# Buffers of their own for the shared loads of a Hyena filter and max-out FFN kernel

## The chip, the core and the metric

The kernel runs on one core of a Trainium2 chip. The metric is the device time of one execution in microseconds (us), the median of several executions. A core has TensorE (PE: matmuls and their weight loads), VectorE (DVE), ScalarE (ACT) and GpSimd (POOL); SyncE (SP) does no arithmetic here and issues most of the transfers. On-chip memory is SBUF; matmuls write to PSUM.

## The reference

Two blocks, one behind the other. The first is a Hyena filter: a small network makes a filter of 12544 positions for each of 128 channels, and the product u = x v of two inputs is convolved with it along the sequence, for 4 batches, by a Fourier transform of twice the length. The second is a feed-forward block with a maximum of three projections.

```python
def _attn_ref(x, v, pos_emb, w1, w2):
    B, S, D = x.shape                       # 4, 12544, 128
    h_mlp = np.maximum(pos_emb @ w1, 0.0) @ w2
    h_filt = h_mlp * np.exp(-0.01 * np.arange(S, dtype=np.float32))[:, None]
    u = x * v
    L = 2 * S
    y = irfft(rfft(u, n=L) * rfft(h_filt, n=L)[None], n=L)[:, :S, :]   # along the sequence
    return x * y

def _moe_ref(x, w1, w2, w3, w_out):         # x: 50176 x 128, d_ff 768
    h = np.maximum(np.maximum(x @ w1, x @ w2), x @ w3)
    return h @ w_out
```

## The kernel before

The transform is done as matmuls. For one batch the work of the convolution is cut into 32 *units* (a piece of both inputs: multiply, turn, first transform) and then 45 *tables* (a pair of frequencies: second transform, product with the filter's spectrum, and the transform back). The convolution of batch b + 1 runs beside the feed-forward block of batch b, step by step in one written order (`manual_schedule`: nothing is reordered). A step, or slot, is one up projection of 392 tokens, 192 steps to a batch.

This is where the conv work of the next batch is put. `s` is the slot in which a unit is joined, or a table's second transform is done; `late` 1 puts an entry behind those with 0 in its slot.

```python
    def conv_steps(b, done):
        ...
        per_pair = 165 / (NK + 0.6 * (NU - done))          # NK = 45 tables, NU = 32 units
        for u in range(done, NU):                          # done: 6 for batch 1, else 0
            s = (u - done) * 0.6 * per_pair + 12
            at(max(0, int(s) - 11), 0, u_load, b, u)
            at(int(s) - 7, 0, u_mul, u)
            at(int(s) - 6, 0, u_planes, u)
            at(int(s) - 5, 0, u_dma, u)
            at(int(s), 0, u_join, u)
            for h in range(2):
                at(int(s + 2 + 0.3 * per_pair * h), 1, u_first, u, h)
        s0 = int((NU - done) * 0.6 * per_pair) + 13
        for g in range(NK):
            s = s0 + int(g * per_pair)
            at(s - 5, 0, w_load, g, 0)
            at(s - 3, 0, h_load, g)
            at(s, 1, g_second, g)
            at(s + 1, 0, g_butterfly, g)
            at(s + 1, 0, w_load, g, 1)
            at(s + 2, 1, g_swap, g)
            at(s + 3, 0, g_re, g)
            at(s + 4, 0, g_im, g)
            at(s + 5, 0, g_sum, g, nc.gpsimd)
            at(s + 7, 0, g_unfold, g)
            at(s + 8, 1, g_third, b, g)
            at(s + 9, 0, g_pair, g)
            at(s + 10, 0, g_store, b, g, nc.gpsimd)
```

The pieces and the buffers that they use. A tile with the same tag in the same pool shares that tag's `bufs` buffers in turn. Unit inputs and tables share the tags `u0` and `u1` of the pool `inq`; a unit's planes share `x` with the spectra `xt`, the turned planes share `xs` with the swapped spectra.

```python
    def u_load(b, u):                                      # xr -> u0, vr -> u1
        ...
            t = pool.tile([P, 512 if pool is inq else 4 * NB], FP32, tag=f"u{len(ts)}", name="ut")
            ...
            nc.sync.dma_start(t, src[4 * g0:4 * g0 + 4, :, c, b, :].rearrange("g p n -> p g n"))
    def u_mul(u):
        a, v = us[u]
        nc.vector.tensor_tensor(out=a, in0=a, in1=v, op=ALU.mult)
    def u_planes(u):                                       # halves of the floats, on GpSimd
        pl_ = cvp.tile([P, 2, 4, P], U16, tag="x", name="planes", bufs=state["xb"])
        ...
    def u_dma(u):                                          # transpose by DMA
        t = cvp.tile([P, 8, P], U16, tag="xs", name="turned", bufs=state["xsb"])
        nc.sync.dma_start_transpose(out=t[:], in_=us.pop(u)[:].rearrange("p h s n -> p (h s n)"))
    def u_join(u): ...                                     # uT <- turned: one half ACT, one DVE
    def u_first(u, h, copy=None): ...                      # matmuls ps <- f, uT; spec <- ps

    def w_load(g, a):                                      # table a = 0 second, 1 third transform
        w = inq.tile([P, 512], FP32, tag=f"u{a}", name="wt")
        nc.sync.dma_start(w[:], wt_d[g, :, a, :])
    def h_load(g): ...                                     # the filter's spectrum, tag uT, SyncE
    def g_butterfly(g):                                    # DVE, writes xt
        xt = state["cv"][0].tile([P, 2, 2, D], FP32, tag="x", name="xt", bufs=state["xb"])
    def g_swap(g):                                         # ACT, xs <- xt
        xs = state["cv"][0].tile([P, 2, 2, D], FP32, tag="xs", name="xs", bufs=state["xsb"])
    def g_re(g): ...                                       # DVE, xt = xt * ht
    def g_im(g): ...                                       # DVE, xs = xs * ht
    def g_sum(g, eng): ...                                 # POOL, xt = xt + xs
    def g_unfold(g):                                       # DVE, ab <- xt
        y = xts.pop(g)
        ab = state["cv"][0].tile([P, 2, 2, D], FP32, tag="ab", name="ab", bufs=2)
        for q, op in enumerate((ALU.add, ALU.subtract)):
            nc.vector.tensor_tensor(out=ab[:, :, q, :], in0=y[:, :, 0, :], in1=y[:, :, 1, :], op=op)
    def g_third(b, g): ...                                 # PE, ps <- ab, wt; then ACT z1 <- ps
```

The pools of the main part, and the step itself:

```python
    hp = ctx.enter_context(tc.tile_pool(name="hp", bufs=3))
    inq = ctx.enter_context(tc.tile_pool(name="inq", bufs=4))     # left over, nothing in it
    utp = ctx.enter_context(tc.tile_pool(name="utq", bufs=3))
    ...
    inq = ctx.enter_context(tc.tile_pool(name="inq", bufs=2))     # the one that is used
    cvp = ctx.enter_context(tc.tile_pool(name="cvp", bufs=3))
    ...
    state = {"turn": cps, "cv": (cvp, cps), "xb": 4, "xsb": 4}

        for j, (name, f) in enumerate(ORDER):              # 12 steps for a pair of token tiles
            if j in loads: bring(k + 1, loads.index(j))    # zt and xT of the next pair, SyncE
            h[name, f] = up(...)                           # pa, relu on ACT; pb, maximum on DVE
            ...
            run(stream.pop(step, ()))                      # down products (ops), sums on GpSimd
            if j in lasts ...: t_last(...)                 # yps, then gt <- yps, xT on DVE
            run(beside.pop(i * NF + j, ()))                # the convolution of the next batch
            step += 1
```

Of the kernel before, what the change touches and what calls it, by code (L numbers as in the profile page):

```python
# [9 lines left out]
FP32 = mybir.dt.float32  # L10
# [5 lines left out]
P = 128  # L16
# [54 lines left out]
def kernel(  # L71
# [16 lines left out]
    NG, _, _, B, NB = x.shape  # L88
    FO, S = posT.shape
    D = w2.shape[1]  # L90
# [226 lines left out]
    inq = None  # L317
# [7 lines left out]
    def pools(b, u):  # L325
        if b == 0:
            return inp0 if u % 2 else inp
        return inp if b == 1 and u < EARLY else inq

    def u_load(b, u):  # L330
        c, g0 = divmod(u, NG // 4)
        ts = []
        for src in (xr, vr):
            pool = pools(b, u)
            t = pool.tile([P, 512 if pool is inq else 4 * NB], FP32, tag=f"u{len(ts)}", name="ut")
            t = t[:, 0:4 * NB].rearrange("p (g n) -> p g n", g=4)
            nc.sync.dma_start(
                t, src[4 * g0:4 * g0 + 4, :, c, b, :].rearrange("g p n -> p g n"))
            ts.append(t)
        us[u] = ts  # L340
# [51 lines left out]

    def w_load(g, a):

        w = inq.tile([P, 512], FP32, tag=f"u{a}", name="wt")
        nc.sync.dma_start(w[:], wt_d[g, :, a, :])
        ws[g, a] = w[:].rearrange("p (k r m) -> p k r m", k=2, r=2)

# [38 lines left out]

    def g_unfold(g):
        y = xts.pop(g)
        ab = state["cv"][0].tile([P, 2, 2, D], FP32, tag="ab", name="ab", bufs=2)  # L440
        for q, op in enumerate((ALU.add, ALU.subtract)):
            nc.vector.tensor_tensor(out=ab[:, :, q, :], in0=y[:, :, 0, :], in1=y[:, :, 1, :],  # L442
                                    op=op)
        abs_[g] = ab
# [30 lines left out]
    def conv_steps(b, done):  # L475


        out = []

        def at(slot, late, fn, *args):  # L480
            out.append((slot, late, len(out), fn, args))

        per_pair = 165 / (NK + 0.6 * (NU - done))
        for u in range(done, NU):
            s = (u - done) * 0.6 * per_pair + 12
            at(max(0, int(s) - 11), 0, u_load, b, u)
            at(int(s) - 7, 0, u_mul, u)
            at(int(s) - 6, 0, u_planes, u)  # L490
            at(int(s) - 5, 0, u_dma, u)
            at(int(s), 0, u_join, u)
            for h in range(2):
                at(int(s + 2 + 0.3 * per_pair * h), 1, u_first, u, h)
# [16 lines that stand above are left out]
        slots = {}  # L511
        for s, _, _, fn, args in sorted(out, key=lambda r: r[:3]):
            slots.setdefault(s, []).append((fn, args))
        return slots
# [194 lines left out]
    warm_up(60)  # L709
    raws.append(load_raw(*jobs[0], nc.sync))  # L710
    u_load(0, 0)
    u_load(0, 1)
    raws.append(load_raw(*jobs[1], nc.sync))
    for u in range(2, 6):
# [11 lines left out]
    for f in range(0, FO, 4):  # L726
        quad([hs[:, f + i] for i in range(4)], f1h[:], specH[:, :, :, f:f + 4])
        u, k = divmod(f // 4, 4)
# [10 lines left out]
    for u in range(0, NU, 2):  # L739
        t = uts.pop(u)  # L740
        for v in range(2):
            if u + 4 < NU:
                u_mul(u + 4 + v)
            at = 4 * (u + v)
# [17 lines left out]
    cvp = pro.enter_context(tc.tile_pool(name="cvp0", bufs=3))  # L762
    cps = pro.enter_context(tc.tile_pool(name="cps0", bufs=3, space=PSUM))
    gps = pro.enter_context(tc.tile_pool(name="gps", bufs=2, space=PSUM))
    sps = pro.enter_context(tc.tile_pool(name="sps", bufs=1, space=PSUM))
    state = {"cv": (cvp, cps), "turn": cps, "xb": 2, "xsb": 2}
    pl = sps.tile([D, 512], FP32, name="pl")
    Gs = {}

# [41 lines left out]
    for s in range(NK + 3):  # L811
# [15 lines left out]
        if 2 <= s <= NK + 1:  # L827
            g_re(s - 2)
            g_im(s - 2)
            g_sum(s - 2, nc.vector)  # L830
            g_unfold(s - 2)
# [28 lines left out]
    inq = ctx.enter_context(tc.tile_pool(name="inq", bufs=4))  # L860
    utp = ctx.enter_context(tc.tile_pool(name="utq", bufs=3))
    f4p = hp.tile([N1, 2, NB // 2], FP32, name="f4p", bufs=1)
    nc.scalar.dma_start(f4p[:], f4p_d)
    inq = ctx.enter_context(tc.tile_pool(name="inq", bufs=2))
    cvp = ctx.enter_context(tc.tile_pool(name="cvp", bufs=3))
    cps = ctx.enter_context(tc.tile_pool(name="cps", bufs=3, space=PSUM))
    hps = ctx.enter_context(tc.tile_pool(name="hps", bufs=3, space=PSUM))
    ops = ctx.enter_context(tc.tile_pool(name="ops", bufs=1, space=PSUM))
    state = {"turn": cps, "cv": (cvp, cps), "xb": 4, "xsb": 4}
    banks = [ops.tile([P, 512], FP32, name=f"ops{i}") for i in range(2)]  # L870


# [25 lines left out]
    for k, (b, i) in enumerate(pairs):  # L898
        if i == 0:
            beside = {}  # L900
            if b + 1 < B:
                beside = conv_steps(b + 1, EARLY if b == 0 else 0)
# [68 lines left out]
```

## Time and profile before

| | |
|---|---|
| time, median of three | 2494.89 us (2493.93 to 2495.22) |
| span of the profiled execution | 2483.4 us |
| mean granted TensorE clock | 0.994 |
| DMA, mean | 165 GB/s |
| feed-forward steps | from 317 us on |

All times in the profile count from the start of the span. A line of the waits reads: engine, line of the kernel that waited, what ended the wait, then the total in us, how often, and the longest. A line of the table by stretches has, for each engine, its busy time and in brackets its instructions. Names such as `ps<-ab,wt` are the tile that is written and those that are read. "issue" means that the profile shows nothing that was waited for. The queue of SyncE is called SPq: its instructions are the issues of transfers, taken in order.

### The profile page before, as it was taken

The numbers are of one execution on the slowest core, as the hardware profiler recorded it, in microseconds if no ns is written. First come the engines' busy times: TensorE is split into PE (matmuls) and PEld (weight loads), VectorE is DVE, ScalarE is ACT, GpSimd is POOL, SyncE is SP. The second block draws the span as 40 slices with busy tenths as digits, with TensorE's granted clock in tenths as the row PEclk, the third lists the DMA queues.
The fourth block names the chain that finished last, engine by engine and source line by source line (L and its number), as shares of the span: only waits on it lengthen the run. The fifth ranks groups of instructions, "written<-read, shape, count | busy, mean of one in ns | idle before, by whom it ended". The sixth has DMA issues, their size and how long they took to land.

```text
span 2483.4 us, 70518 instructions
## 1 busy us (share of the span) xinstructions
PE 2370.5 (95%) x29025; PEld 1650.3 (66%) x29025; DVE 1623.6 (65%) x3044; ACT 1007.7 (41%) x1981; POOL 1388.5 (56%) x1595
## 2 busy tenths in 40 slices
PE   9999999999999899999999999998999999999999
PEld 8988867766666566666666666765666666666665
DVE  5588756576777747668887855658878873333333
ACT  2688834434334324434443423443344432222222
POOL 2022246566656666646665667646666665555565
PEclk9999999999999999999999999999999999999999
DMA  7789879767677559957877749966877853222221
GB/s 171 173 251 277 248 160 190 152 181 205 177 192 209 155 119 201 181 132 204 216 199 197 209 114 178 185 148 176 215 204 200 211 136 91 51 67 60 54 73 21
DMA packets 459274, 408.66 MB, mean 165 GB/s; under 512 B 322660, under 2 KB 338333, under 8 KB 458953
## 3 DMA queue, kind: packets, MB, share of 16 engines
q1 hardware_dynamic: 417664, 315.23, 53.9%
q0 software_dynamic: 28464, 75.72, 10.9%
q10 hardware_dynamic: 12825, 13.21, 1.7%
q8 instruction: 228, 3.74, 0.6%
q14 instruction: 93, 0.76, 0.1%
HBM read 295.76 MB, written 84.67 MB: 153 GB/s over the span
## 4 chain that ended last, share of the span: by engine, by line
PE 81%; DVE 11%; issue 3%; DMA 2%; ACT 1%; POOL 1%; SPq 0%; DVEq 0%; POOLq 0%; ACTq 0%
PE pa L131 17%; PE pb L131 17%; PE ops L622 17%; PE ps L131 12%; PE ps L140 7%; DVE ab L442 5%; PE yps L131 5%; PE sps L796 3%; DVE hid L576 2%; DVE zs L468 1%; DVE xt L430 1%; DVE xs L433 1%; PE pm L304 1%; PE gps L782 1%; PE pst L349 1%
## 5 line engine op out<-in xcount | busy, mean ns | idle before, releaser
L576 DVE TENSOR_TENSOR hid<-hid,pb 128x392 f32<-128x392 f32 x768 | 428.5, 558 | 504.3 <-PE pb L131 434.2
L573 ACT ACTIVATE hid<-pa 128x392 f32<-128x392 f32 x768 | 382.1, 497 | 715.0 <-PE pa L131 694.4
L131 PE MATMUL pa<-gt,w_sb 128*64 128x392 f32 x3072 | 642.0, 496 | 0.5 <-DVE hid L576 0.4
L131 PE MATMUL pb<-gt,w_sb 128*64 128x392 f32 x3072 | 639.0, 494 | 3.0 <-ACT hid L573 3.0
L131 PEld LDWEIGHTS pb<-gt,w_sb 128*64 128x64 f32 x3072 | 221.0, 137 | 293.7 <-issue 268.3
L622 PE MATMUL ops<-hid,wo_sb 128*64 128x196 f32 x3072 | 330.3, 328 | 0.0
L647 POOL DMA_DIRECT2D out_dram<-o x256 | 162.0, 637 | 280.5 <-DVE o L642 110.3
L622 PEld LDWEIGHTS ops<-hid,wo_sb 128*64 128x64 f32 x3072 | 220.2, 136 | 138.3 <-issue 113.8
L131 PE MATMUL ps<-ab,wt 128*64 128x128 f32 x2880 | 205.0, 280 | 86.9 <-DVE ab L442 84.1
L592 POOL TENSOR_TENSOR s<-hid 128x392 f32<-128x392 f32 x192 | 206.7, 1076 | 135.9 <-DVE hid L576 109.6
L592 POOL TENSOR_TENSOR s<-hid,s 128x392 f32<-128x392 f32 x192 | 201.0, 1047 | 99.3 <-DVE hid L576 97.2
L442 DVE TENSOR_TENSOR ab<-xt 128x256 f32<-128x256 f32 x360 | 252.2, 740 | 1.6
L131 PEld LDWEIGHTS ps<-ab,wt 128*64 128x64 f32 x2880 | 161.3, 137 | 130.8 <-DVE ab L442 110.2
L592 POOL TENSOR_TENSOR hid<-hid,s 128x392 f32<-128x392 f32 x192 | 204.8, 1073 | 42.9 <-DVE hid L576 24.5
L436 POOL TENSOR_TENSOR xt<-xt,xs 128x512 f32<-128x512 f32 x135 | 172.2, 1275 | 96.6 <-DVE xs L433 80.2
L131 PEld LDWEIGHTS pa<-gt,w_sb 128*64 128x64 f32 x3072 | 200.5, 138 | 21.2 <-issue 2.0
L430 DVE TENSOR_TENSOR xt<-xt,ht 128x512 f32<-128x512 f32 x180 | 201.7, 1121 | 14.3 <-ACT ht L801 14.1
L592 POOL TENSOR_TENSOR hid<-hid 128x392 f32<-128x392 f32 x192 | 203.2, 1077 | 0.2
L131 PE MATMUL ps<-spec,wt 128*64 128x128 f32 x2880 | 190.1, 274 | 2.1 <-issue 2.1
L140 PE MATMUL ps<-f,uT 98*64 98x90 f32 x4096 | 188.0, 242 | 4.3 <-DVE spec L144 3.1
L140 PEld LDWEIGHTS ps<-f,uT 98*64 98x64 f32 x4096 | 176.7, 137 | 13.6 <-ACT spec L144 4.0
L622 PE MATMUL ops<-s,tw 128*64 128x196 f32 x1536 | 170.8, 329 | 0.0
(105 smaller groups left out, 3067.7 us busy)
## 6 DMA issues: line engine op xcount, KB each, us to landing
wt<-wt_const SPq DMA_DIRECT2D x360, 256.0 KB, 4.6
ht<-hd SPq DMA_DIRECT2D x270, 256.0 KB, 5.0
zd<-zs POOLq DMA_DIRECT2D x135, 256.0 KB, 4.0
zt<-zd SPq DMA_DIRECT2D x192, 180.0 KB, 4.1
ut<-in_xr_dram SPq DMA_DIRECT2D x128, 196.0 KB, 3.5
ut<-in_vr_dram SPq DMA_DIRECT2D x128, 196.0 KB, 4.0
xT<-in_x_dram SPq DMA_DIRECT2D x256, 98.0 KB, 4.1
out_dram<-o POOLq DMA_DIRECT2D x256, 98.0 KB, 3.3
```

The source lines that it names most:

```text
L131: nc.tensor.matmul(out[64 * h:64 * h + 64], lhsT[:, 64 * h:64 * h + 64], rhs, start=start, stop=stop, skip_group_check=True)
L140: nc.tensor.matmul(ps[64 * c:64 * c + 64, 256 * i + r * N1:256 * i + (r + 1) * N1], a[:, r, :], table[:, c * N1:(c + 1) * N1], start=(i % ...
L304: nc.tensor.matmul(ps[64 * h:64 * h + HH, 512 * r + q * FO:512 * r + (q + 1) * FO], posv[64 * h:64 * h + 64, P - 1 - 2 * (8 * i + q) - r, ...
L430: nc.vector.tensor_tensor(out=xt[:], in0=xt[:], in1=hts[g][:, 0], op=ALU.mult)
L436: eng.tensor_tensor(out=xts[g][:], in0=xts[g][:], in1=xss.pop(g)[:], op=ALU.add)
L442: nc.vector.tensor_tensor(out=ab[:, :, q, :], in0=y[:, :, 0, :], in1=y[:, :, 1, :], op=op)
L573: nc.scalar.activation(h[:], pa[:, 0:N], Relu)
L576: nc.vector.tensor_tensor(out=h[:], in0=h[:], in1=pb[:, 0:N], op=ALU.max)
L592: nc.gpsimd.tensor_tensor(out=out[:], in0=a[:], in1=b[:], op=op)
L622: nc.tensor.matmul(ps[64 * c:64 * c + 64, 0:H2], w, rhs[:, :, c, :], start=start, stop=True, skip_group_check=True)
L647: nc.gpsimd.dma_start(dst[64 * m:64 * m + 64, 4 * i + c:4 * i + 8:2, b, :], t[m][64 * c:64 * c + 64].rearrange("d k (q n) -> d (k q) n", q=2))
L796: nc.tensor.matmul(ps[64 * h:64 * h + 64, (2 * c + k) * 2 * D:(2 * c + k + 1) * 2 * D], G[:, k, c], w2x[:].rearrange("p s d -> p (s d)"), ...
```

## The change

The tags `u0` and `u1` get four and three buffers in place of two each, and the pool that had nothing in it is no longer opened beside the one in use (its four was what the writer had meant to have). That takes 7 x 2 KB in place of 4 x 2 KB in each partition. It is paid for by one buffer less for `x` and for `xs` (three in place of four, 2 KB each) and one for `ab` (one in place of two, 2 KB). So that three buffers of planes last, a unit's steps from load to transpose come one slot later. The aim is that SyncE's queue, which takes its entries in order, no longer stands before a load whose buffer is in use. The arithmetic stays as it was; the prologue keeps its two buffers of `ab`.

```diff
 def u_load(b, u):
-            t = pool.tile([P, 512 if pool is inq else 4 * NB], FP32, tag=f"u{len(ts)}", name="ut")
+            t = pool.tile([P, 512 if pool is inq else 4 * NB], FP32, tag=f"u{len(ts)}", name="ut",
+                          bufs=4 - len(ts) if pool is inq else 3)
 def w_load(g, a):
-        w = inq.tile([P, 512], FP32, tag=f"u{a}", name="wt")
+        w = inq.tile([P, 512], FP32, tag=f"u{a}", name="wt", bufs=4 - a)
 def g_unfold(g):
-        ab = state["cv"][0].tile([P, 2, 2, D], FP32, tag="ab", name="ab", bufs=2)
+        ab = state["cv"][0].tile([P, 2, 2, D], FP32, tag="ab", name="ab",
+                                    bufs=state["abb"])
 def conv_steps(b, done):
-            at(max(0, int(s) - 11), 0, u_load, b, u)
-            at(int(s) - 7, 0, u_mul, u)
-            at(int(s) - 6, 0, u_planes, u)
-            at(int(s) - 5, 0, u_dma, u)
+            at(max(0, int(s) - 10), 0, u_load, b, u)
+            at(int(s) - 6, 0, u_mul, u)
+            at(int(s) - 5, 0, u_planes, u)
+            at(int(s) - 4, 0, u_dma, u)
 # prologue
-    state = {"cv": (cvp, cps), "turn": cps, "xb": 2, "xsb": 2}
+    state = {"cv": (cvp, cps), "turn": cps, "xb": 2, "xsb": 2, "abb": 2}
 # main part
-    inq = ctx.enter_context(tc.tile_pool(name="inq", bufs=2))
-    state = {"turn": cps, "cv": (cvp, cps), "xb": 4, "xsb": 4}
+    state = {"turn": cps, "cv": (cvp, cps), "xb": 3, "xsb": 3, "abb": 1}
```

## The prediction

> **What bounds the kernel now.** I read, in this order: the engine table of the page, the table by stretches, TensorE's waits, the waits of the DMA queue that SyncE issues on, VectorE's waits, and one stretch of the timeline. The first question is how much time TensorE is not working, since nothing else can be won.
>
> ```profile
> PE 2370.5 (95%) x29025; PEld 1650.3 (66%) x29025; DVE 1623.6 (65%) x3044; ACT 1007.7 (41%) x1981; POOL 1388.5 (56%) x1595
> ```
>
> TensorE is busy for 95% of the span, so all its idle time is 113 us. Next, the same by stretch. I cut the part from 325 us on where the last `uT` and the last `ab` matmuls stand: three times a unit stretch (inputs of the next batch multiplied, turned, transformed), then a table stretch (spectra times filter and back), then the last batch with no convolution beside it.
>
> ```profile
> core 0: us, PE busy (x) PEld busy (x) DVE busy (x) ACT busy (x) POOL busy (x), PEclk, DMA share, GB/s
> 325.00:480.00 155.00, 154.31 (x1997) 106.07 (x1995) 92.20 (x164) 60.79 (x118) 93.08 (x119) 1.00 0.86 166
> 480.00:880.00 400.00, 372.60 (x4175) 257.22 (x4172) 294.66 (x561) 157.96 (x328) 250.93 (x260) 0.99 0.70 183
> 880.00:1080.00 200.00, 196.45 (x2588) 133.79 (x2586) 121.70 (x209) 76.50 (x149) 125.79 (x161) 1.00 0.85 169
> 1080.00:1460.00 380.00, 350.20 (x4042) 238.52 (x4040) 306.07 (x550) 153.50 (x321) 240.68 (x250) 0.99 0.73 190
> 1460.00:1662.00 202.00, 197.00 (x2582) 134.34 (x2580) 117.67 (x210) 75.31 (x148) 126.93 (x160) 0.99 0.86 168
> 1662.00:2041.00 379.00, 349.61 (x4048) 237.93 (x4046) 305.06 (x550) 154.00 (x322) 241.01 (x250) 1.00 0.72 190
> 2041.00:2470.00 429.00, 429.00 (x4276) 262.50 (x4274) 154.88 (x316) 109.44 (x232) 240.72 (x267) 1.00 0.24 61
> ```
>
> Stretch minus first column is TensorE's idle time: 0.7, 3.6 and 5.0 us in the unit stretches (9.2 together), 27.4, 29.8 and 29.4 us in the table stretches (86.6), nothing in the last. Who ends those waits, over 325 to 2470 us:
>
> ```profile
> PE ps L131 <- DVE ab L442: 83.4, 65, 4.6
> PE ps L131 <- issue: 3.8, 4, 1.7
> PE ps L140 <- DVE spec L144: 3.1, 2, 2.1
> PE pb L131 <- ACT hid L573: 3.0, 6, 0.6
> PE ps L140 <- ACT spec L144: 1.2, 2, 0.6
> ```
>
> So 83.4 of some 96 us is the third matmul waiting for the unfolded sums; no line names a DMA. The queue that the change is about, meanwhile, waits a great deal (325 to 2041 us):
>
> ```profile
> SPq L396 <- PE ps L131: 641.9, 129, 12.7
> SPq L337 <- POOL planes L365: 115.8, 49, 11.3
> ```
>
> L396 is the load of a table, L337 the load of a unit: both stand before a buffer that is still in use, and everything behind them in the queue stands too. Whether that harms anybody is told by the engines' waits for landings. VectorE's, same stretch:
>
> ```profile
> DVE gt L563 <- PE ops L622: 80.1, 27, 4.2
> ...
> DVE ut L344 <- DMA ut<-in_vr_dram: 26.0, 21, 2.5
> ...
> DVE ut L344 <- POOL planes L364: 6.1, 4, 2.9
> DVE gt L563 <- DMA ht<-hd: 5.9, 2, 2.9
> ```
>
> Late units cost VectorE 26.0 us. The last line I do not believe: `gt` reads no `ht`. At 1901.1 us the timeline shows it starting just as the `linx` product ends, which reads the `gt` of two pairs before; that is the wait of the first line (a `gt` buffer not free) under another name. Tables and filters therefore cause no wait on an engine.
>
> **What the Trainium skill says.** "SBUF — State Buffer", section "Who interferes with whom": a VectorE instruction with two SBUF inputs contends with a GpSimd instruction that reads SBUF, and the second to issue is blocked until the first is done. The trace agrees, and it is the cause of the 83.4 us:
>
> ```profile
> 1885.31 4.20 DVE L442 TENSOR_TENSOR ab<-xt 128x256 f32<-128x256 f32 x2
> ```
>
> Two unfolds, 418 ns each at the median, take 4.20 us here, while GpSimd runs its sums without a pause from 1884.69 to 1888.88 us. The same section says that a DMA never contends with a compute engine; no wait above speaks against it, so earlier transfers should not slow VectorE. "PSUM — Partial Sum Buffer", section "Engine vs sequencer instructions", says that ScalarE, VectorE and GpSimd are strictly in order; so one late unit holds all VectorE work behind it, and that is how a load could reach TensorE at all.
>
> **The change, part by part.** Slots are steps of the up projection: 768 of them between 317 and 2470 us, 2.8 us each. A unit follows the last after 0.6 x 165/(45 + 0.6 x 32) = 1.54 slots (1.63 for batch 1), a table after 2.57 (2.72).
>
> *Tables.* The second table is loaded at s+1 and read at s+8: 7/2.57 = 2.7, so it needs three buffers and had two. That is the 641.9 us. With three (and four for the first table, which needs 5/2.57 = 1.9) this wait nearly vanishes from the queue. On an engine it saves 0 us, because none waited for what stood behind it.
>
> *Units.* The input that becomes the product lives from its load to `planes`, the other to the multiplication: before, 5 and 4 slots, so 3.2 and 2.6 buffers, out of two. Hence the 115.8 us, and a load asked for at s-11 goes out at about s-7. With four and three it can go out when asked for, now s-10. The multiplication moves from s-7 to s-6, still 4 slots, 11 us, after the load, against a landing of 3.7 us at the median: the 26.0 us go. The transpose moves from s-5 to s-4 on paper; in the trace of before it is issued at s-1 to s-3, held up behind unit loads, and lands 4.3 us later. Without the blocking it should be earlier than before, not later.
>
> *Fewer buffers.* Spectra: `x` is written at s+1 and last read at s+7, 6/2.57 = 2.3, three suffice; moreover writer and last reader are both VectorE, in order. `xs` lives 3 slots there. Transposed planes: issued s-4, joined at s, 4/1.54 = 2.6, again three. Before, 5/1.54 = 3.2 needed four; this is why the steps were moved by one. Unfolded sums with one buffer: the unfold of g+1 comes at least 9 slots after s(g), the reading matmul is at s(g)+8, and VectorE reaches the next slot only after a maximum that waits for a TensorE product issued behind that matmul. So no new wait: 0 us.
>
> *Instruction streams.* The order on TensorE is unchanged. On the other engines only unit steps move past neighbours; in the table stretches nothing moves. No work is added or removed.
>
> *The sum.* Table stretches: 0 of 86.6 us, since neither the order, nor VectorE's sharing with GpSimd, nor any landing changes. Unit stretches: at most 9.2 us. Of that 0.7 us in each (2.1) is "issue" at the seam to the tables, untouched. Of the other 7.1 us, the waits for `spec` by VectorE and for `hid` by VectorE (1.0 in the second stretch, 2.1 + 0.4 in the third) fall among late units and late transposes at the start of the stretch: 3.5 us, which should go. The rest, 3.6 us, returns at the same places of both stretches (984 and 1567, 1054 and 1637 us) and looks like rhythm; I give it half, 1.8. Together 5.3 us: 2494.9 - 5.3 = 2489.6, called 2490.
>
> **Rivals.**
> One: the blocked queue costs more than the waits show, and unblocking it relieves the table stretches. For it speaks the sheer 641.9 us and the `ht` lines. Against it: no engine's wait there names a landing that it needs. If true, up to half of the 86.6 us could go: some 2450.
> Two: one of the reduced buffers turns into a wait. For it: `ab` at one buffer has no slack in number, only in order, and it feeds the very matmul that waits most. If each of 135 tables lost 0.3 us, it would be 40 us: 2535. Against it: the argument from order above.
> Three: moving the multiplication and the planes by a slot puts them beside other GpSimd sums, and blocked VectorE instructions appear elsewhere. `ut` already ranges from 535 to 2916 ns. It can go either way, a few us, in stretches where TensorE has little to lose: 2485 to 2498.
>
> **Range and chances.** The three runs of before lie within 1.3 us, so a few us can be seen. All the idle time that I think in reach bounds the gain: 2495 - 9 = 2486; allowing for a little of rival one, 2482 at the low end. At the high end, rival three without the gain: 2497. Faster by over 2% would need 50 us, over half of the table stretches' idle time: 1.5%. Slower by over 2% needs rival two in full: 1%. Within 2%: 97.5%.
>
> **What will show it.** Right: the queue's wait for the second table falls from 641.9 us to under 100, that for `planes` from 115.8 to under 30; VectorE's wait for the second unit input falls from 26.0 to under 5; idle TensorE time in the unit stretches falls from 9.2 to about 4, and in the table stretches stays at 87 within 3. Wrong: another figure for the 83.4 us of waits for `ab`, in either direction; a wait of `ab` for the third matmul on VectorE; a wait of `uT` for the transposed planes longer than 7.2 us, which would mean that the later transposes are too late.

## The result, and the profile after

| | before | changed |
|---|---|---|
| time, median | 2494.46 us (2493.93 to 2495.22, 4 runs) | 2480.68 us (2478.76 to 2482.35, 4 runs) |
| ratio to before | | 0.9944, 95% interval 0.9927 to 0.9962 |
| the same, timed in turns on another chip | 2492.14 us (32 runs) | 2482.39 us (5 runs), ratio 0.9950, 0.9937 to 0.9963 |

The change gains 10 to 14 us, 0.5%. The prediction had the right place and a gain of 5.3 us: the measured time lies 1.3 us below its range, that of the second row at the range's low end. A ratio, here and below, is the record's own estimate from all runs, with its interval; it can differ by a thousandth or so from the quotient of the medians (0.9961 in the second row).

The engine table of the changed kernel's page, first line (busy us, share of the span, instructions):

```profile
PE 2373.3 (96%) x29025; PEld 1655.7 (67%) x29025; DVE 1628.5 (66%) x3044; ACT 1008.8 (41%) x1981; POOL 1395.9 (56%) x1595
```

The table by stretches of the changed kernel, cut at the same times as in the prediction; the first two columns are the length and TensorE's busy time:

```profile
325.00:480.00 155.00, 155.00 (x1990) 107.60 (x1986) 92.88 (x162) 60.14 (x116) 92.32 (x118) 0.98 0.91 172
480.00:880.00 400.00, 372.22 (x4177) 257.90 (x4176) 294.00 (x558) 158.05 (x328) 252.16 (x261) 0.99 0.70 182
880.00:1080.00 200.00, 197.47 (x2602) 134.64 (x2604) 120.38 (x214) 76.66 (x149) 130.71 (x162) 1.00 0.90 173
1080.00:1460.00 380.00, 350.18 (x4046) 238.34 (x4043) 306.03 (x549) 153.89 (x320) 240.01 (x249) 0.99 0.71 188
1460.00:1662.00 202.00, 200.13 (x2632) 136.96 (x2634) 125.27 (x217) 78.06 (x153) 129.96 (x162) 1.00 0.87 175
1662.00:2041.00 379.00, 349.48 (x4038) 237.34 (x4035) 305.92 (x551) 153.15 (x319) 241.21 (x251) 0.99 0.70 186
```

TensorE's idle time (length less its busy time) is 0, 2.5 and 1.9 us in the unit stretches, 4.4 in place of 9.2. In the table stretches it is 27.8, 29.8 and 29.5 us, together 87.1 in place of 86.6: nothing has moved there. The waits for the sums are the same too (TensorE's waits, 325 to 2470 us, changed kernel):

```profile
PE ps L131 <- DVE ab L444: 83.9, 64, 4.6
...
PE ps L140 <- ACT spec L144: 2.3, 4, 0.6
...
PE pb L131 <- ACT hid L575: 0.6, 2, 0.3
```

What is gone is the wait for `spec` by VectorE (3.1 us), and most of that for `hid` by ScalarE (3.0 to 0.6); the wait for `spec` by ScalarE rose from 1.2 to 2.3. And SyncE's queue, 325 to 2041 us, in the changed kernel:

```profile
SPq L404 <- DVE xs L434: 263.5, 55, 12.2
SPq L404 <- DVE hid L578: 232.6, 46, 9.2
SPq L397 <- PE ps L131: 113.3, 38, 9.4
```

The wait did not go away, it moved one load on. L397, the table, falls from 641.9 to 113.3 us, and L404, the load of the filter's spectrum, stands for some 500 us: its three buffers are now the ones that are short. The queue, let past one full pool, ran on to the next one; that it waits says nothing until an engine waits for it. Of the signs that the prediction had set for being right, this is the one that missed (113.3 us against under 100). The others came: no wait of a unit load for `planes` is left (115.8 before), nor one of VectorE for the second unit input (26.0), and ScalarE's for turned planes is 1.4 us.

To see where the time came from I took, in each trace, the starts of the first product of the feed-forward part, of each table stretch (first `ps<-spec,wt`) and of each unit stretch (last `ps<-ab,wt`), and subtracted. U and T are the unit and table stretches; all in us:

```
                     start   U1     T1     U2     T2     U3     T3     rest   U2 + U3
before               316.7   160.0  400.3  200.8  381.1  201.9  379.1  443.5   402.7
before, once more    320.0   160.9  402.4  204.3  381.5  201.5  379.8  443.5   405.8
changed              320.4   160.3  400.6  198.4  380.8  196.5  380.3  443.3   394.9
changed, once more   320.6   160.4  400.1  198.4  381.0  197.0  380.1  443.3   395.4
```

The second and third unit stretches are 7.3 to 10.9 us shorter together, and the rest is level within what two executions of one kernel differ by. That is where the gain lies.

### The profile page after: what moved, and what is told of

Read it like the earlier page. It is cut to its first block, busy times and chain, and to the rows that moved or that the text cites. A ratio compares the mean times of both kernels' runs of the same rounds, so it can differ in the third digit from the quotient of the medians.

```text
span 2480.6 us, 70451 instructions
## 1 busy us (share of the span) xinstructions
PE 2373.3 (96%) x29025; PEld 1655.7 (67%) x29025; DVE 1628.5 (66%) x3044; ACT 1008.8 (41%) x1981; POOL 1395.9 (56%) x1595
## 4 chain that ended last, share of the span: by engine, by line
PE 81%; DVE 11%; DMA 4%; issue 2%; ACT 1%; SPq 0%; ACTq 0%; POOL 0%; DVEq 0%; POOLq 0%
PE pb L131 17%; PE pa L131 17%; PE ops L624 17%; PE ps L131 12%; PE ps L140 7%; PE yps L131 5%; DVE ab L444 4%; PE sps L798 3%; DMA ht<-hd 3%; DVE hid L578 2%; DVE zs L470 1%; DVE xs L434 1%; PE pm L304 1%; PE gps L784 1%; DVE xt L431 1%
## 5 line engine op out<-in xcount | busy, mean ns | idle before, releaser
L594 POOL TENSOR_TENSOR hid<-hid 128x392 f32<-128x392 f32 x192 | 209.8, 1111 | 0.2
```

The source lines that it names most:

```text
L594: nc.gpsimd.tensor_tensor(out=out[:], in0=a[:], in1=b[:], op=op)
```

## The experiments

Each kernel was timed in turns with the kernel before on one chip; ratios are to that. "On the changed kernel" says what the edit was made to.

**The changed kernel again, and the kernel before profiled again.** No edit.

> The changed kernel once more, timed in turns with the kernel before on one chip. Theory A: what the two traces show is the whole gain. From the first product of the feed-forward part to the end they differ by 6.5 us (2166.7 to 2160.2), and the 13.8 us between the medians is made larger by conditions, since the timed runs of before lay 9.6 us above its own profiled run: ratio 0.997, about 7 us. Theory B: the 13.8 us are the change's, and the profiled execution of before was a lucky one: ratio 0.9945 again.

Measured: 2482.39 us, ratio 0.9950 (0.9937 to 0.9963). The interval holds theory B's 0.9945 and not theory A's 0.997; the medians are 9.8 us apart, between A's 7 and B's 13.8.

> The kernel before, profiled once more: 32 timed executions of it have a mean of 2492.4 us, and the profiled one took 2485.3. If that profile was of an untypical execution, this one takes some 2489 to 2494 us, its feed-forward part starts at 320 us and not at 317 (as in five other profiles), and it has more stretches of half clock than the eight of the first. If the first was typical, 2485 us again, and the profiler itself makes it faster.

Measured: 2495.73 us, feed-forward part from 320.0 us, thirteen stretches of half clock in place of eight. The mean granted clock of this execution and of the first profile of before (the view of the cores, same line of each):

```profile
core 0: 2493.9 us, clock 0.988
```

```profile
core 0: 2483.4 us, clock 0.994
```

So the profile that the prediction was read from was of an unusually quick execution, at 2485.3 us below all 32 timed in turns with the changed kernel (2486.8 to 2496.2), as theory B had it: against this one its prologue was 3.3 us shorter, its tables 3.3 us, and its U2 and U3 3.1 us. This one in turn was longer than most, 3.6 us above their median. A typical execution lies between the two, and so does the measured gain: U2 and U3 shrank by 7.3 to 10.9 us, the medians differ by 9.8.

**Only the later steps.** On the kernel before:

```diff
-            at(max(0, int(s) - 11), 0, u_load, b, u)      # and -7, -6, -5 to -6, -5, -4
+            at(max(0, int(s) - 10), 0, u_load, b, u)
```

> The kernel before with the unit steps one slot later and nothing else. If the gain comes from the new places of the steps (what stands beside what on VectorE and GpSimd), it appears here: 7 us or more. If it comes from loads that no longer stand in the queue, nothing is gained here, and the transposes, still held up, land later against their joins: 0 to 6 us slower than before.

Measured: 2488.15 us, ratio 0.9986 (0.9978 to 0.9994): 4 us faster, although VectorE waits longer for unit inputs (34.3 us in place of 26.0) and ScalarE and VectorE now wait 58.8 us for transposes (7.2 before). Neither expectation holds; the steps' places have a share of their own. U2 and U3 are 399.9 us long.

**Only fewer buffers.** On the kernel before:

```diff
-    state = {"turn": cps, "cv": (cvp, cps), "xb": 4, "xsb": 4}        # ab: bufs=2
+    state = {"turn": cps, "cv": (cvp, cps), "xb": 3, "xsb": 3, "abb": 1}
```

> The kernel before with three spectra, three swapped ones and one of the unfolded sums, without the new load buffers. If fewer buffers cost nothing, as predicted for the table stretches, 0 us; in the unit stretches planes and turned planes now wait for transposes that are still held up, which may cost 2 to 8 us. If one buffer of unfolded sums costs something, 20 us or more, in the table stretches.

Measured: 2495.49 us, ratio 1.0010 (1.0002 to 1.0018), 3.4 us slower. Its table stretches (398.5, 380.5 and 381.1 us) are those of before, so the single buffer of sums is free, as the argument from order had it. In the unit stretches GpSimd now waits 84.5 us, in place of 7.0, for planes that a held-up transpose has not released. That this wait makes the 3.4 us is not shown: in the one execution that was profiled, a quick one, U2 and U3 are 404.2 us, within those of before.

**The second load tag back to two.** On the changed kernel:

```diff
-                          bufs=4 - len(ts) if pool is inq else 3)     # tables: bufs=4 - a
+                          bufs=4 - 2 * len(ts) if pool is inq else 3) # tables: bufs=4 - 2 * a
```

> The changed kernel with four buffers for the first tag and only two for the second, so that the second table waits in the queue as before. Theory A (the table wait is harmless): the queue's wait for the second table is back at some 600 us and the time is that of the changed kernel within 2 us, or at most 3 us more where unit inputs are a little late. Rival: the freed table loads made the gain; then the time goes back to that of before, 7 to 14 us more.

Measured: 2483.09 us, ratio 0.9957 (0.9945 to 0.9969), the changed kernel's time within 1 to 2 us. Yet in its queue (325 to 2041 us) the table waits nearly as long as ever:

```profile
SPq L397 <- PE ps L131: 609.4, 118, 12.8
```

The largest wait in the queue of the kernel before was worth nothing in this schedule. This is the prediction's first rival, and it is out.

**The first load tag back to two.** On the changed kernel:

```diff
-                          bufs=4 - len(ts) if pool is inq else 3)     # tables: bufs=4 - a
+                          bufs=2 + len(ts) if pool is inq else 3)     # tables: bufs=2 + a
```

> The changed kernel with only two buffers for the first tag (unit inputs that become the product, first tables) and three for the second. If it is the unit loads behind the planes that mattered, this gives most of the gain back, down to what the later steps alone gained: 5 to 8 us slower than the changed kernel, the queue's wait for planes at 100 us or more, VectorE's wait for unit inputs at 25 us or more. If not, within 2 us of the changed kernel.

Measured: 2492.97 us, ratio 0.9998 (0.9986 to 1.0010): all of the gain is gone. Who waits for a landing in that kernel, over 325 to 2041 us (the lines of unit inputs and of transposed planes):

```profile
POOL planes L365 <- DMA turned<-planes: 96.0, 43, 7.5
...
ACT uT L381 <- DMA turned<-planes: 63.0, 31, 6.5
...
DVE ut L345 <- DMA ut<-in_vr_dram: 34.7, 26, 3.2
...
DVE uT L381 <- DMA turned<-planes: 17.9, 10, 4.3
```

In the changed kernel the same four stand at 14.0, 1.4, 0 and 0 us. The table stretches are those of the changed kernel (1161.2 us in all, 1161.7 there), U2 and U3 are 404.7 us, as before the change. So of seven buffers for loads it is the four of the first tag that pay, and they pay for the unit inputs and not for the first tables.

**Late inputs and late transposes, one at a time.** On the changed kernel:

```diff
-            at(max(0, int(s) - 10), 0, u_load, b, u)
+            at(max(0, int(s) - 8), 0, u_load, b, u)
```

> The changed kernel with the unit inputs loaded two slots before the multiplication in place of four, about where they really went out before. If late inputs are the cost, VectorE waits for them again (20 us or more) and the time is 4 to 10 us above that of the changed kernel. If held-up transposes are the cost, VectorE waits, but TensorE hardly notices: 0 to 3 us.

Measured: 2492.11 us, ratio 1.0000 (0.9989 to 1.0011), the time of before to the digit; U2 and U3 are 404.6 us again. VectorE's wait for the inputs of units in it:

```profile
DVE ut L345 <- DMA ut<-in_vr_dram: 71.9, 28, 6.6
```

The other edit, again on the changed kernel:

```diff
-            at(int(s) - 4, 0, u_dma, u)
+            at(int(s) - 2, 0, u_dma, u)
```

> The changed kernel with the transpose issued two slots before its join in place of four. If held-up transposes are the cost, this brings them back with everything else of the change in place: 4 to 10 us slower than the changed kernel, TensorE idle in the unit stretches up from 4 to 8 us or more. If unit inputs are the cost, within 2 us of it.

Measured: 2488.58 us, ratio 0.9982 (0.9972 to 0.9991), 6 us slower than the changed kernel. Here VectorE does not wait for inputs at all; ScalarE and VectorE wait 88.1 us for transposes. Either delay alone is enough to lose most or all of the gain. But both are larger than what the kernel before had, which waited 26.0 us for inputs and 7.2 for transposes, and the totals of these waits do not rank the kernels: with only the later steps they are 34.3 and 58.8 us, and that kernel is 4 us faster than before. How much of the loss in the kernel before went by each link is not shown.

**Transposes from ScalarE's queue.** On the kernel before:

```diff
-        nc.sync.dma_start_transpose(
+        nc.scalar.dma_start_transpose(
```

> The kernel before, with the transposing transfers issued by ScalarE's queue in place of SyncE's; all buffers and steps as before. A transpose then no longer stands behind a unit load that waits for a buffer. If held-up transposes are what cost time before, this gains most of the change's 10 us: 5 to 10 us faster, less what their issue takes from ScalarE (90 times 1.3 us, in stretches where ScalarE is busy for 38 to 40%). If late unit inputs cost it, VectorE still waits some 20 us for them and the gain is below 3 us.

Measured: 2505.08 us, ratio 1.0051 (1.0032 to 1.0070), 13 us slower. No wait for transposes is left, but VectorE waits 75.8 us for unit inputs in place of 26.0. It doesn't tell the two links apart, since it worsened the other one.

**The steps back in place, with the new buffers.** On the changed kernel, the four lines of unit steps as before:

```diff
-            at(int(s) - 4, 0, u_dma, u)                   # load -10, mul -6, planes -5
+            at(int(s) - 5, 0, u_dma, u)                   # load -11, mul -7, planes -6
```

> The changed kernel with the unit steps back where they were before (load s-11, multiply s-7, planes s-6, transpose s-5), all buffers as changed. If the new load buffers are what gains, and the later steps only spare a buffer, the time is that of the changed kernel within 2 us: a transpose now waits for a buffer of turned planes until about s-4, where the change puts it. If the later steps take a share of their own (moved alone, they gained 3.6 us on the means), it is 3 to 5 us slower than the changed kernel.

Measured: 2485.17 us, ratio 0.9971 (0.9961 to 0.9981), 3 to 5 us slower than the changed kernel. Its GpSimd waits 47.5 us for planes that a transpose still reads, in place of 14.0; that is the landing wait that grew most. It doesn't explain the loss by itself: with the second load tag at two buffers the same wait is 43.4 us, and there the time is the changed kernel's. What the later steps gain by is open.

**The third matmul one slot later.** Two kernels that touch what the change left alone. The first, on the changed kernel:

```diff
+            n = int(g < NK - 1)                           # NK - 1: the last table of a batch
-            at(s + 8, 1, g_third, b, g)                   # pair s + 9, store s + 10
+            at(s + 8 + n, 1, g_third, b, g)               # pair s + 9 + n, store s + 10 + n
-    state = {..., "abb": 1}                               # load tags: 4 and 3 buffers
+    state = {..., "abb": 2}                               # load tags: 4 and 2 buffers
```

> What neither kernel touches: the third matmul waits 84 us for unfolded sums that VectorE, blocked by GpSimd, brings late. Here it comes one slot later (last table of a batch excepted), with two buffers for the sums, paid for by the second load tag going from three to two, which cost nothing. If the wait is only a matter of the distance between unfold and use, most of the 84 us goes: 40 to 80 us faster than the changed kernel. If VectorE is the bound of the table stretches (busy for 306 of 380 us, the blocked time counted), the wait turns up at another tile: 0 to 20 us.

Measured: 2462.72 us, ratio 0.9896 (0.9874 to 0.9917), by the ratios 13, by the medians 18 to 20 us below the changed kernel, at most half of the least expected if the distance were all. TensorE's waits, 325 to 2470 us, in this kernel:

```profile
PE ps L131 <- DMA wt<-wt_const: 47.8, 26, 3.4
PE ps L131 <- DVE ab L444: 10.6, 8, 2.1
```

The wait for sums has fallen from 83.9 to 10.6 us. In its place TensorE waits for a table, always the first (all 26 waits stand before a second transform): a later third matmul holds the second table a slot longer, with two buffers the queue stands before it, and the next first table stands behind. What was worth nothing before is now the bound. The second kernel gives both load tags three buffers, on the first:

```diff
-                          bufs=4 - 2 * len(ts) if pool is inq else 3) # tables: bufs=4 - 2 * a
+                          bufs=3)                                     # tables: bufs=3
```

> As the kernel with the later third matmul, but three buffers for both load tags in place of four and two. In that kernel TensorE waits 47.8 us for first tables that stand in the queue behind a second table whose buffer is in use. If the queue was all that kept the gain down, this takes that wait away: 20 to 40 us below 2462.7 us, with unit inputs still on time (a unit needs 3.2 buffers of the first tag, so its load goes out about 3 slots before the multiplication). If VectorE is the bound behind it, 0 to 10 us, and the third matmul waits for the sums again.

Measured: 2404.89 us (2403.20 to 2406.57), ratio 0.9661 (0.9647 to 0.9676): 84 us below the kernel before and 58 below the last one, more than expected. TensorE is busy for 98% of the span; its first two waits (325 to 2470 us):

```profile
PE ps L131 <- DVE xt L157: 9.2, 5, 1.8
PE ps L131 <- DVE ab L444: 7.0, 7, 1.8
```

Three of each without the later matmul was not run, nor the later matmul with one buffer for the sums. The table stretches are 371.5, 358.6 and 357.3 us long, 74 us less than in the changed kernel, though TensorE's idle time in them fell by 56 us only (87.1 to 30.9); the unit stretches (U2 + U3 393.6) stay. The unfolds are held up as before (419 ns at the median, up to 4891; 289 us in all, 266 in the kernel before); the slot of distance hides it.

## Why the prediction was wrong, by its own steps

- *Tables, 0 us*: right. The table stretches kept their waits to half a microsecond, and putting the table's queue wait back (609.4 us) cost nothing. But "this wait nearly vanishes from the queue" was only half so: it fell to 113.3 us, and some 500 us went to the filter loads.
- *Fewer buffers, 0 us for the sums*: right, alone and together. For the planes it was right only with the other parts: alone, the fewer buffers cost 3.4 us.
- *Units, inputs on time*: right. The load goes out at s-8.0 at the median of batches 2 and 3 (s-7.5 before, a slot counted from its first product), not at the s-10 that I wrote, since the queue is still held up by other loads; but it lands 5.6 us ahead of the multiplication, in place of 1.1, and VectorE's 26.0 us are gone.
- *Units, transposes earlier than before*: wrong. They go out at s-2.7 at the median, as before (s-2.6). What left is the tail at the start of a stretch: of the 64 units of batches 2 and 3, two were joined within 0.1 us of the landing, in place of five.
- *The sum, 5.3 us*: this is the step that failed, in its size. It turned TensorE's idle time into time one for one, and took the 9.2 us that one trace showed as the bound ("At most 9.2 us"). As a sum of idle time it was nearly right: "from 9.2 to about 4" was forecast, 4.4 came. But U2 and U3 shrank by more. Here they are taken apart, cut at the same matmuls (us, the last column from unrounded values):

```
                     U2 + U3   TensorE idle   at half clock   U2 + U3 - idle - half of the half clock
before                 402.7        8.6            3.4            392.4
before, once more      405.8       10.0            6.8            392.4
changed                394.9        3.7            0              391.2
changed, once more     395.4        4.1            0              391.4
```

  Of the 7.8 us between the first and the third line, 4.8 are idle time. Half of the 3.4 us at half clock, 1.7, was lost while TensorE counted as busy, just behind a wait (the last section shows it); that the last column is level within 1.3 us speaks for counting it so. The other 1.2 us stay open. And the first line is of a quick execution: against the second line 10.9 us went, 6.3 of them idle time and 3.4 half clock.
- *Rival one* is refuted by the second tag at two buffers. *Rival two* by the fewer buffers alone. *Rival three* was half right: the later steps have an effect of their own, some 4 us in this kernel's favour, alone as well as on top. What brings it stays open in both places: alone, the waits for landings rose and the time fell; on top, GpSimd's wait for planes fell, but another kernel has that wait at no cost.

The prediction took the range of the three runs of before (1.3 us) for their spread, and passed over that the profiled run lay 9.6 us below them. An execution that differs by so much can have other waits (in U2 and U3 8.6 us idle, against 10.0 in the second), and the low end of the range should have allowed for it.

## What to carry to other kernels

Idle time that can be won is no bound on the gain, where the clock falls behind a wait: here it was 62% of it (4.8 of 7.8 us) in the units. A long wait of a transfer queue is no cost until an engine waits for what stands behind it; count the buffers that a tile needs as slots held over slots between two, and give them to the chain that an engine waits for, here the unit inputs and not the tables with their 642 us. When such a wait is left alone because it is free, look again after the next change: with the third matmul moved, two buffers for the second table cost 58 us (2462.7 against 2404.9 us with three of each, the first tag having one less). And a blocked instruction need not be made faster, if its user can come one slot later and there is a buffer for it.

## What the runs showed of the hardware

The granted clock of TensorE falls to half for 3.4 us, at times for two or three times that. Two places of the trace of before, by short stretches (the value after the instruction counts is the granted clock). Around 1531 us, where TensorE had stood 2.07 us for `spec`:

```profile
1528.02:1531.44 3.42, 1.35 (x42) 1.17 (x38) 2.78 (x5) 0.47 (x1) 3.15 (x5) 1.00 1.22 252
1531.44:1534.85 3.41, 3.41 (x24) 2.16 (x26) 2.05 (x5) 0.27 (x1) 2.81 (x5) 0.50 1.17 230
```

Around 1207 us, where it stood 1.95 us for `ab`:

```profile
1203.75:1207.17 3.42, 2.70 (x26) 1.47 (x22) 2.65 (x7) 0.07 (x2) 1.11 (x2) 1.00 0.72 156
1207.17:1210.58 3.41, 2.18 (x34) 1.92 (x36) 3.18 (x6) 2.10 (x5) 3.40 (x5) 1.00 0.54 137
1210.58:1213.99 3.41, 3.41 (x54) 2.32 (x52) 2.78 (x5) 0.82 (x2) 1.56 (x3) 1.00 0.75 192
```

In the second row TensorE is busy all the time, at half clock: a wait of 2 us has cost more behind it, and it shows as busy time. Behind the wait at 1207 us nothing of the kind follows. What decides is where a wait lies. The half-clock stretches of one trace start whole multiples of 3.413 us apart (from one to the next in before: 89, 34, 107, 64, 61 and 46), so each execution has a fixed grid, and the rows above are cut on it. The first wait lies in one window of the grid and leaves it 2.07 us idle; the second falls on a boundary, and leaves 0.72 us in one window and 1.23 in the next. Over the 14 traces, from 330 us to 12 us before the end, half clock followed each of the 51 windows at full clock that were idle for over 2.01 us, 37 of the 58 idle for 1.8 to 2.01 us, and one of the 8536 below 1.8 us. The Trainium skill, "TensorE: Matmul & The Clock Gate", section "What's actually happening", tells of half rate after an idle window of about 3.4 us. The window's length agrees, but it need not be idle throughout: here 1.8 to 2.0 us of it were enough.

Whole executions differ along with this: 32 of the kernel before range from 2486.8 to 2496.2 us, and over them a thousandth less of mean clock goes with 1.6 us more. That the place of the grid against the program makes this spread is likely, but not shown.
